# Loads of 62 KB a partition, V cut to fill them, and K one head ahead near the end, in a DMA-fed decode kernel

## The chip, the cores and the metric

The kernel runs on one core of one Trainium2 chip. The metric is device time in microseconds (us), the median of several runs; lower is better.

## What is computed

One decode step, fp32 throughout, with two tokens (B = 2, one query each, D = 512). The input x is layer-normed to xn, and the result is the sum of three terms:

```python
def _A_ref(x, k_cache, v_cache, wq, wo):           # 32 heads of 128, window W = 2048
    q = (x @ wq).reshape(B, Sq, Hq, Dh).transpose(0, 2, 1, 3)
    k = k_cache[:, :, Sk - W:, :]; v = v_cache[:, :, Sk - W:, :]
    scores = einsum("bhqd,bhkd->bhqk", q, k) * (Dh ** -0.5)
    o = einsum("bhqk,bhkd->bhqd", softmax(scores), v)
    return o.transpose(0, 2, 1, 3).reshape(B, Sq, Hq * Dh) @ wo
def _B_ref(x, w_gate, w_up, w_down):               # F = 1376, no nonlinearity
    return ((x @ w_gate) * (x @ w_up)) @ w_down
return x + _A_ref(xn, ...) + _B_ref(xn, ...)
```

Only the last 2048 positions of the K and V caches are read. Every byte of K, V and the weights is used once.

## The kernel before, in words

**The stream.** Before the launch, all inputs but a small rest are laid out in one long array, `stream`, in the order in which they will be loaded. `blocks()` (line 47) is that order: a list of loads, each a list of fields, and each field a kind, an index and a width in fp32 elements a partition. The kinds are `k` and `v` (one head's K or V for both tokens, CK = 4096 elements, which is 16 KB a partition), `wq` (a quarter of the query weights of a group of four heads, 512), `wo` (one head's output weights, 512), `wg`/`wu` (gate and up weights, in two halves), `wd`, `wh` (chunks and half chunks of w_down, 512 and 256), `wr` (the x term and a few rest rows of w_down) and `vh` (one token's half of the last head's V).

**The buffers.** A load goes into a `step` tile of STEP elements a partition; STEP is three units of 4608, so 13,824 elements, 54 KB. There are three such buffers (`BUFS = 3`). `pump()` (line 150) issues the next load on SP as soon as a buffer is free in program order, and `done()` (line 173) strikes off a field when the instruction that uses it has been written; when the last field of a load is struck off, the buffer is free and `pump()` is called. On the chip the DMA instruction on SP then waits on the engines that read the old contents. A load of the steady part holds exactly three units, either K, V, K or V, K, V of successive heads with their `wq` and `wo`; V runs three heads behind K (LAG = 3). Loads that share a buffer's key at the end (the last V's and the w_down pieces) are separate DMAs into one buffer. The 25-row rest of w_down goes to the tile `wd_tail` by one more DMA on SP (line 187), issued behind the first three loads.

**One head.** For each K, VectorE (DVE) multiplies K by the broadcast query (`products`, line 278) and sums over the head dimension (`sums`, 286); `maxima` (291) takes the maximum on DVE and over the partitions on GpSimd (POOL); `weights` (299) makes the exponentials on ScalarE (ACT) and sums them on POOL; `reciprocals` (314) runs on DVE. For V, TensorE (PE) multiplies the weights with V (`weigh`, 330: 8 pieces of 512 columns, two matmul records for each, as fp32), ACT copies the sum out of PSUM (`copy_out`, 339), PE transposes it (`transpose`, 346) and ACT scales it into `oT`, and PE multiplies by `wo` into `acc` (`project_o`, 365). `pv` (373) does the weighing of one or two heads and the copy, `values` (379) the whole of it. PE also makes the queries of coming heads (`project_q`, 261) and the gate and up products (395). Each engine runs its instructions in the order written (class `InOrder`, whose line 102 therefore stands for nearly all instructions in the profile).

**The order.** The main loop (line 471) goes through the loads of `blocks()`: for each K of the load it does the head's work, and the `values` of the load's V heads come after the first K's sums. It breaks off ahead of the loads that hold V of head 27. Then the end is written out by hand (lines 496 to 548): head 30's products and sums, `values` of heads 26 and 27, head 31's products, then V of heads 28 to 31 as they land, with `down(n)` (432) for chunks of w_down, and `keep_busy(n)` (327), a matmul whose result nothing uses, in PE's waits. Line 508 puts a copy of the accumulator in a tile of its own, `acc_sb`, ahead of a new accumulation over four column groups. The last five loads are: half of V 31; `wo` 31 with w_down chunks 4 to 6; chunk 7 with the first half chunk; two half chunks; the last half chunk (`down_half`, 443). The result is copied by DVE (`o_out`) and written by one DMA.

Of the kernel before, what the change touches and what calls it, by code (L numbers as in the profile page):

```python
# [8 lines left out]
F32 = mybir.dt.float32  # L9
# [7 lines left out]
P = 128  # L17
B, D, H, DH, SK, F = 2, 512, 32, 128, 8192, 1376
# [6 lines left out]
FR = F - NFC * P  # L25
FH = [(0, 2 * FB), (2 * FB, F)]
LAG = 3
M = B
OUT = P

# [2 lines left out]
JG = J // 4  # L33
CK, CQ, CO = B * J * DH, NC * GC, D
CP = CQ // NC
UNIT = CK + max(CP, CO)
STEP = 3 * UNIT
WD = [(0, 2), (2, 4), (4, 7), (7, 8)]
HD = D // 2
HP = P // 2  # L40
NT, FT, FP = 2, 25, 28
FX = FR - NT * FT
RX = M + FX
PADS = 96, 248


def blocks():

    def wd(n):
        return [("wd", i, D) for i in range(*WD[n])]

    def k(h):
        return [("k", h, CK)] + ([("wq", h, CP)] if h + HG < H else [])  # L60

    def v(h):
        return [("v", h, CK), ("wo", h, CO)]

    def gu(half):
        n = NC * (FH[half][1] - FH[half][0])
        return [("wg", half, n), ("wu", half, n)]

    units = []
    for h in range(LAG, H - 1):  # L70
        units += [k(h), v(h - LAG)]
    ones = [("pick", 0, 8 * B), ("rows", 0, NFB * B)]
    first = [("x", 0, B * NC)] + ones + [("w", 0, NC * DH)]
    loads = [[("w", 1, CQ - NC * DH)] + k(0) + k(1), gu(0) + k(2)]
    loads += [gu(1) + units[0] + units[1] + wd(0) + [("wr", 0, HD)]]
    loads += [sum(units[i : i + 3], []) for i in range(2, len(units), 3)]
    loads += [k(H - 1) + v(H - 1 - LAG) + wd(1)]
    out = [(("f", 0), first)] + [(("s", i), fields) for i, fields in enumerate(loads)]
    late, last = ("s", len(loads)), ("s", len(loads) + 1)
    out += [(late, v(H - 3) + [("vh", 0, CK // B)]), (late, v(H - 2))]  # L80
    out += [(last, [("vh", 1, CK // B)]), (last, [("wo", H - 1, CO)] + wd(2))]
    halves = [("wh", (c, n), HD) for c in range(WD[-1][1], NFC) for n in range(2)]
    out += [(last, wd(3) + halves[:1])]
    return out + [(last, halves[i : i + 2]) for i in range(1, len(halves), 2)]


class InOrder:
# [30 lines left out]
def kernel(  # L118
# [65 lines left out]
    pick = got["pick", 0][0].rearrange("p (r s b) -> p r s b", s=2, b=B)  # L184
    rows = got["rows", 0][0]

    sp.dma_start(wd_tail[FP : FP + FT, :], tail)
    carry = rows[:M, :M]

    mean_w = const.tile([P, P], F32, name="mean_w")  # L190
# [43 lines left out]
        xnb, xn.rearrange("p c b -> p (c b)").unsqueeze(2).to_broadcast([P, NC * B, P])  # L234
    )

    q_ps, s_t, mm_t, p_t, sum_t, rec_t, o_sbs, oT = {}, {}, {}, {}, {}, {}, {}, {}
    n_acc = bank = 0

    def side(h):  # L240
# [89 lines left out]
    def weigh(h, v, parts, first, last):  # L330

        for n, part in enumerate(parts):
            b, i = divmod(part, JG)
            pe.matmul(
                o_ps[bank][32 * i : 32 * i + 8 * B, :], p_t[h][:, b, i, :],
                v[:, FB * n : FB * (n + 1)], start=first and b == 0, stop=last and b == B - 1,
            )

    def copy_out():
        nonlocal bank  # L340
        o_sb = small.tile([P, 4 * DH], F32, name="o_sb", bufs=2)
        act.copy(o_sb, o_ps[bank])
        bank = 1 - bank
        return o_sb

    def transpose(heads, o_sb):
        d = tr[:, 8 + 4 * bank : 12 + 4 * bank]
# [24 lines left out]

    def pv(heads):
        for h in heads:
            weigh(h, got["v", h][0], range(CK // FB), h == heads[0], h == heads[-1])
            done("v", h)
        return copy_out()

    def values(heads, busy=((), ())):
        o_sb = pv(heads)  # L380
        for n in busy[0]:
            keep_busy(n)
        transpose(heads, o_sb)
        for n in busy[1]:
            keep_busy(n)
        for h in heads:
            project_o(h)

# [79 lines left out]
    spare_in = xnb.rearrange("p a b -> p (a b)")  # L468
    for i in range(2):
        project_first(i)  # L470
    for _, fields in blocks():
        ks = [i for kind, i, _ in fields if kind == "k"]
        vs = [i for kind, i, _ in fields if kind == "v"]
        if vs and vs[-1] >= H - 5:
            break
# [26 lines left out]
    maxima(h)  # L502
    reciprocals(h - 1)
# [24 lines left out]
    project_o(H - 3)  # L528
    reciprocals(h + 1)
    keep_busy(P)  # L530
    weigh(H - 2, got["v", H - 2][0], range(CK // FB), False, False)
    done("v", H - 2)
    keep_busy(192)
    weigh(H - 1, got["vh", 1][0], range(JG, B * JG), False, True)
    done("vh", 1)
# [17 lines left out]
def laid_out(x):  # L553
# [29 lines left out]
    def field(kind, i):  # L583
        if kind in first:
            return first[kind]
        if kind in ("k", "v"):
            return cache[kind][i].reshape(P, CK)
        if kind == "w":
# [56 lines left out]
```

## Time and profile before

| what | value |
|---|---|
| time, median of 3 runs | 377.35 us (377.3 to 377.47) |
| the profiled execution's own time | 377.36 us |
| its span, first to last instruction | 375.5 us |
| mean granted TensorE clock | 0.805 |
| PE, DVE, ACT, POOL busy | 256.6, 294.5, 58.2, 25.2 us |
| read from HBM | 159.50 MB |

The profile is one execution. Its busy shares are averages over the whole span. The DMA share of a stretch is the mean busy share of the core's 16 DMA engines. A packet row counts every transfer that a DMA engine made, data and the 4-byte semaphore writes behind it. The "us to landing" of an issue runs from the start of the instruction on SP to the last engine's end of that load, so it includes the time in the queue behind earlier loads. PEld is the weight load of a matmul; where matmuls follow closely, its start times are the finer clock of PE's progress.

### The profile page before, as it was taken

To read this page: it belongs to the slowest core of one execution; us is meant where nothing else is said; L and a number is where in the kernel's file an instruction comes from. 1 tells how busy PE (TensorE), PEld (TensorE's weight loads), DVE (VectorE), ACT (ScalarE), POOL (GpSimd) and SP (SyncE) were. 2 spreads that over 40 slices of the span, in tenths; PEclk is the share of its full clock that TensorE was granted. 3 is DMA by queue.
4 is the path that set the end of the run, shared out by engine and by line. 5 is a ranking of instruction groups with operands and counts; after the bars stand their busy time and mean duration, and the time that the engine had idled before them with its cause. 6 is when DMAs were issued, how large, how long until landed. Compare 5 with 4: busy or idle time off the path is not lost.

```text
span 375.5 us, 2881 instructions
## 1 busy us (share of the span) xinstructions
PE 256.6 (68%) x1100; PEld 87.3 (23%) x1100; DVE 294.5 (78%) x145; ACT 58.2 (16%) x260; POOL 25.2 (7%) x74
## 2 busy tenths in 40 slices
PE   3386586988648486854858675385847768646996
PEld 3241123232112122211222122121212123012343
DVE  4299691998599499869949976994997799599950
ACT  1011002122020211201112020111202021121131
POOL 1001000000000000000000100000000000000010
PEclk9996988889896666889766698875869688556999
DMA  8999999999999999999999999999999999999995
GB/s 323 468 436 450 401 440 442 412 459 427 425 442 418 448 442 412 443 430 436 448 407 449 430 424 454 414 443 436 418 459 418 432 445 431 430 420 435 418 413 237
DMA packets 4506, 159.73 MB, mean 425 GB/s; under 512 B 501, under 2 KB 757, under 8 KB 1166
## 3 DMA queue, kind: packets, MB, share of 16 engines
q1 hardware_dynamic: 4494, 159.57, 98.6%
q8 instruction: 8, 0.13, 0.1%
q14 instruction: 4, 0.03, 0.0%
HBM read 159.50 MB, written 0.07 MB: 425 GB/s over the span
## 4 chain that ended last, share of the span: by engine, by line
DMA 62%; PE 18%; DVE 17%; ACT 2%; issue 1%; SPq 0%; DVEq 0%
DMA step<-in_stream_dram 62%; DVE step L102 8%; DVE s L102 8%; PE o_ps L102 6%; PE q L102 4%; PE acc L102 4%; PE tr L102 3%; ACT o_sb L102 1%; ACT oT L102 1%; SPq L102 0%; ACT hT L102 0%; DVE o_sb L102 0%; DVE m L102 0%; ACT hX L102 0%; DVE o_out L102 0%
## 5 line engine op out<-in xcount | busy, mean ns | idle before, releaser
L102 DVE TENSOR_TENSOR step<-step,q 128x4096 f32<-128x4096 f32 x31 | 136.6, 4407 | 53.2 <-DMA step<-in_stream_dram 53.2
L102 PE MATMUL q<-step,xnb 128*128 128x512 f32 (+1 forms) x128 | 93.0, 877 | 74.8 <-DMA step<-in_stream_dram 74.8
L102 DVE TENSOR_REDUCE s<-step 128x32 f32<-128x4096 f32 x32 | 141.4, 4419 | 1.1
L102 PE MATMUL o_ps<-step,p 128*16 128x512 f32 x512 | 69.8, 680 | 10.3 <-DMA step<-in_stream_dram 10.3
L102 PEld LDWEIGHTS q<-step,xnb 128*128 128x128 f32 x128 | 32.5, 276 | 129.4 <-DMA step<-in_stream_dram 75.3
L102 PE MATMUL acc<-step,oT 128*2 128x512 f32 (+1 forms) x88 | 35.1, 553 | 9.1 <-ACT oT L102 9.1
L102 PE MATMUL tr<-first,o_sb 128*128 128x2 f32 (+4 forms) x192 | 26.6, 257 | 15.9 <-ACT o_sb L102 12.8
L102 ACT COPY o_sb<-o_ps 128x512 f32<-128x512 f32 x23 | 13.5, 585 | 149.2 <-PE o_ps L102 149.2
L102 PEld LDWEIGHTS tr<-first,o_sb 128*128 128x128 f32 (+2 forms) x192 | 24.2, 195 | 37.0 <-ACT o_sb L102 31.8
L296 POOL PARTITION_ALL_REDUCE mm<-m x32 | 11.3, 354 | 282.9 <-DVE rec L102 177.7
L102 PEld LDWEIGHTS o_ps<-step,p 128*16 128x16 f32 x512 | 13.3, 106 | 70.3 <-issue 53.3
L102 ACT ACTIVATE nm<-mm 128x2 f32<-128x2 f32 x32 | 6.5, 203 | 126.2 <-POOL mm L296 126.2
L102 ACT ACTIVATE p<-s,nm 128x16 f32<-128x16 f32 x64 | 19.2, 300 | 1.0
L312 POOL PARTITION_ALL_REDUCE sum<-rs x32 | 12.7, 398 | 55.5 <-ACT p L102 55.5
L102 ACT ACTIVATE oT<-tr,rec 128x1 f32<-128x1 f32 x64 | 12.1, 260 | 26.6 <-PE tr L102 26.6
L102 PE MATMUL o_ps<-step,xn 128*2 128x512 f32 (+1 forms) x48 | 12.6, 575 | 0.0
L102 DVE TENSOR_TENSOR step<-step,tr 128x4096 f32<-128x4096 f32 x1 | 4.4, 4421 | 9.6 <-DMA step<-in_stream_dram 9.6
L102 ACT ACTIVATION_READ_ACCUMULATOR p<-s,nm 128x1 f32 x64 | 11.9, 186 | 0.0
L102 PE MATMUL q<-xnb,mean_w 128*128 128x512 f32 (+4 forms) x24 | 9.4, 487 | 0.0
L102 PEld LDWEIGHTS acc<-step,oT 128*2 128x2 f32 x88 | 3.9, 83 | 18.7 <-ACT oT L102 14.5
L102 PE MATMUL acc<-step,hT 128*2 128x128 f32 (+2 forms) x72 | 7.1, 306 | 0.0
L102 DVE COPY o_out<-acc 128x128 f32<-128x128 f32 x1 | 0.3, 292 | 8.5 <-PE acc L102 8.5
(40 smaller groups left out, 44.3 us busy)
## 6 DMA issues: line engine op xcount, KB each, us to landing
step<-in_stream_dram SPq DMA_DIRECT2D x16, 6912.0 KB, 33.6
step<-in_stream_dram SPq DMA_DIRECT2D x2, 6656.0 KB, 37.2
step<-in_stream_dram SPq DMA_DIRECT2D x2, 6400.0 KB, 32.8
step<-in_stream_dram SPq DMA_DIRECT2D x1, 5376.0 KB, 15.5
step<-in_stream_dram SPq DMA_DIRECT2D x1, 4864.0 KB, 29.8
step<-in_stream_dram SPq DMA_DIRECT2D x1, 3328.0 KB, 16.9
step<-in_stream_dram SPq DMA_DIRECT2D x1, 2304.0 KB, 22.0
step<-in_stream_dram SPq DMA_DIRECT2D x2, 1024.0 KB, 16.8
```

Of the source, the lines that this page charges most:

```text
L102: made = call(*args, **kwargs)
L296: nc.gpsimd.partition_all_reduce(mm, m, P, bass_isa.ReduceOp.max)
L312: nc.gpsimd.partition_all_reduce(sum_t[h], rs, P, bass_isa.ReduceOp.add)
```

## The change

- STEP is 31 blocks of 512 elements: 15,872 elements, 62 KB a partition (63,488 bytes). The three buffers stay three.
- A new function `packed` fills each steady load to exactly STEP. It takes fields from the queue in order, skips one that doesn't fit for a later one that does, and cuts a V (in pieces of 512 columns) where only a part fits. A field of kind `v` is now keyed by head and range of pieces; `weigh_all` multiplies the pieces of one head, and strikes each off by itself.
- From head EARLY = 27 on, K goes one place earlier in the order of the stream; `groups()` writes the loop's order of heads apart from the loads, and `values` of the group with head 27 comes at the group's end. Heads 28 and 29 get a loop of their own, and V of head 25 moves to the part written by hand, where `transpose` gets a `slot`.
- The first loads are put together anew: queries and K 0, 1, 2; gate and up weights with K 3; V 0, w_down and K 4, V 1.
- At the end, chunk 7 of w_down and three half chunks are one load (5,120 bytes a partition) in place of two (3,072 and 2,048); `project_o` of head 30 goes ahead of `down(3)`. Of the calls of `keep_busy` around V of heads 26 and 27, two of 512 columns fall away.
- `wd_tail` is loaded by five DMAs of five rows in place of one of 25, and `acc_sb` takes a buffer of the `o_sb` pool.

The loads by bytes a partition: before 2,168 (first), 43,008, 51,200, 53,248, sixteen of 55,296, 51,200, 53,248, 38,912, 26,624, 18,432, 8,192, 8,192, 3,072, 2,048, 1,024: 30 loads. After: 2,168, 61,440, 62,464, 60,416, fifteen of 63,488, 38,912, 26,624, 18,432, 8,192, 8,192, 5,120, 1,024: 26 loads. Both sum to 1,245,304 bytes a partition. After, ten V heads are cut in two (3, 7, 8, 10, 12, 15, 19, 22, 23, 25).

```diff
-UNIT = CK + max(CP, CO)
-STEP = 3 * UNIT
+BLK = CO
+STEP = 31 * BLK
...
+def packed(queue):
+    loads = []
+    while queue:
+        load, room = [], STEP
+        while queue and room:
+            n = next((n for n, f in enumerate(queue) if f[2] <= room or f[0] == "v"), None)
+            if n is None:
+                break
+            kind, i, w = queue.pop(n)
+            if w > room:
+                h, p0, p1 = i
+                cut = p0 + room // FB
+                queue.insert(n, (kind, (h, cut, p1), (p1 - cut) * FB))
+                i, w = (h, p0, cut), room
+            load.append((kind, i, w))
+            room -= w
+        loads.append(load)
+    return loads
+
+def groups():
+    units = [u for h in range(LAG, H - 1) for u in (("k", h), ("v", h - LAG))]
+    parts = [[("k", 0), ("k", 1)], [("k", 2)], units[:2]]
+    parts += [units[i : i + 3] for i in range(2, len(units), 3)]
+    return [[[i for kind, i in p if kind == want] for want in "kv"] for p in parts]
...
-    loads = [[("w", 1, CQ - NC * DH)] + k(0) + k(1), gu(0) + k(2)]
-    loads += [gu(1) + units[0] + units[1] + wd(0) + [("wr", 0, HD)]]
-    loads += [sum(units[i : i + 3], []) for i in range(2, len(units), 3)]
+    loads = [[("w", 1, CQ - NC * DH)] + k(0) + k(1) + k(2), gu(0) + k(3) + gu(1)]
+    loads += [v(0) + wd(0) + [("wr", 0, HD)] + k(LAG + 1) + v(1)]
+    order = [(h - (h >= EARLY), k, h) for h in range(LAG + 2, H - 1)]
+    order += [(h + 0.5, v, h - LAG) for h in range(LAG + 2, H - 1)]
+    order.sort(key=lambda n: n[0])
+    loads += packed([f for _, fields, h in order for f in fields(h)])
...
-    out += [(last, wd(3) + halves[:1])]
-    return out + [(last, halves[i : i + 2]) for i in range(1, len(halves), 2)]
+    return out + [(last, wd(3) + halves[:-1]), (last, halves[-1:])]
...
-    sp.dma_start(wd_tail[FP : FP + FT, :], tail)
+    for i in range(0, FT, FT // TS):
+        sp.dma_start(wd_tail[FP + i : FP + i + FT // TS, :], tail[i : i + FT // TS, :])
...
+    def weigh_all(h, first, last):
+        for kind, i in [key for key in got if key[0] == "v" and key[1][0] == h]:
+            weigh(h, got[kind, i][0], range(i[1], i[2]), first, last)
+            done(kind, i)
...
-            if vs and n == 0:
+            if vs and n == 0 and h < EARLY:
                 values(vs)
...
+            if h == EARLY:
+                values(vs)
+
+    for h in (H - 4, H - 3):
+        products(h)
+        sums(h)
+        maxima(h)
+        weights(h)
+        reciprocals(h - 1)
...
-    values([H - 6, H - 5], ((GC, 256), (GC,)))
+    o_sbs = pv([H - 7]), pv([H - 6, H - 5])
+    transpose([H - 7], o_sbs[0], 1 - bank)
+    transpose([H - 6, H - 5], o_sbs[1])
+    keep_busy(256)
+    for i in range(H - 7, HF):
+        project_o(i)
     keep_busy(GC)
...
-    acc_sb = const.tile([M, D], F32, name="acc_sb")
+    acc_sb = small.tile([P, D], F32, name="o_sb", bufs=2)[:M, :]
...
     down(2)
     project_o(H - 1)
+    project_o(H - 2)
     down(3)
-    project_o(H - 2)
```

More of the change, by code (lines that the diff above doesn't have):

```diff
@@ L27 @@
 LAG = 3
+EARLY = 27
 M = B
@@ L40 @@
 HP = P // 2
-NT, FT, FP = 2, 25, 28
+NT, FT, FP, TS = 2, 25, 28, 5
 FX = FR - NT * FT
@@ L44, with k, v @@
 PADS = 96, 248
+def k(h):
+    return [("k", h, CK)] + ([("wq", h, CP)] if h + HG < H else [])
+def v(h):
+    return [("v", (h, 0, CK // FB), CK), ("wo", h, CO)]
+def packed(queue):
[21 more added lines that the diff above has]
+    return [[[i for kind, i in p if kind == want] for want in "kv"] for p in parts]
 def blocks():
@@ L57, in wd @@
         return [("wd", i, D) for i in range(*WD[n])]
[L59 to L63, printed above, removed]
     def gu(half):
@@ L67, in gu @@
         return [("wg", half, n), ("wu", half, n)]
-    units = []
-    for h in range(LAG, H - 1):
-        units += [k(h), v(h - LAG)]
     ones = [("pick", 0, 8 * B), ("rows", 0, NFB * B)]
     first = [("x", 0, B * NC)] + ones + [("w", 0, NC * DH)]
-    loads = [[("w", 1, CQ - NC * DH)] + k(0) + k(1), gu(0) + k(2)]
-    loads += [gu(1) + units[0] + units[1] + wd(0) + [("wr", 0, HD)]]
-    loads += [sum(units[i : i + 3], []) for i in range(2, len(units), 3)]
+    loads = [[("w", 1, CQ - NC * DH)] + k(0) + k(1) + k(2), gu(0) + k(3) + gu(1)]
[4 more added lines that the diff above has]
+    loads += packed([f for _, fields, h in order for f in fields(h)])
     loads += [k(H - 1) + v(H - 1 - LAG) + wd(1)]
@@ L235 @@
     )
-    q_ps, s_t, mm_t, p_t, sum_t, rec_t, o_sbs, oT = {}, {}, {}, {}, {}, {}, {}, {}
+    q_ps, s_t, mm_t, p_t, sum_t, rec_t, oT = {}, {}, {}, {}, {}, {}, {}
     n_acc = bank = 0
@@ L344, in copy_out, with transpose @@
         return o_sb
-    def transpose(heads, o_sb):
-        d = tr[:, 8 + 4 * bank : 12 + 4 * bank]
+    def transpose(heads, o_sb, slot=None):
+        slot = bank if slot is None else slot
+        d = tr[:, 8 + 4 * slot : 12 + 4 * slot]
         s0, s1 = side(heads[0]), side(heads[-1]) + 1
@@ L374, in pv, with values @@
         for h in heads:
-            weigh(h, got["v", h][0], range(CK // FB), h == heads[0], h == heads[-1])
-            done("v", h)
+            weigh_all(h, h == heads[0], h == heads[-1])
         return copy_out()
[L379 to L385, printed above, removed]
+    def values(heads):
+        transpose(heads, pv(heads))
         for h in heads:
@@ L470 @@
         project_first(i)
[L471 to L475, printed above, removed]
+    for ks, vs in groups()[:-2]:
         for n, h in enumerate(ks):
@@ L530 @@
     keep_busy(P)
-    weigh(H - 2, got["v", H - 2][0], range(CK // FB), False, False)
-    done("v", H - 2)
+    weigh_all(H - 2, False, False)
     keep_busy(192)
@@ L585, in field @@
             return first[kind]
-        if kind in ("k", "v"):
+        if kind == "k":
             return cache[kind][i].reshape(P, CK)
+        if kind == "v":
+            h, p0, p1 = i
+            return cache[kind][h].reshape(P, CK)[:, p0 * FB : p1 * FB]
         if kind == "w":
```

## The prediction, as it stood before the result

> **What bounds the kernel now.** I read the page's strip of slices and its DMA queues first. The DMA line holds nine tenths or more from the second slice to the last but one, and one hardware queue takes nearly all of the span.
>
> ```profile
> span 375.5 us, 2881 instructions
> DMA  8999999999999999999999999999999999999995
> q1 hardware_dynamic: 4494, 159.57, 98.6%
> DMA 62%; PE 18%; DVE 17%; ACT 2%; issue 1%; SPq 0%; DVEq 0%
> ```
>
> A mean can hide holes, so I cut the span into windows (busy us of PE, PEld, DVE, ACT, POOL, then clock, DMA share, GB/s), and asked the DMA view for the even stretch from 130 to 310 us, where only 54 KB loads are in flight, and for the last small loads.
>
> ```profile
> 20.00:60.00 40.00, 28.42 (x86) 9.66 (x84) 33.37 (x16) 5.30 (x22) 2.61 (x7) 0.87 1.00 430
> 100.00:140.00 40.00, 26.37 (x109) 7.94 (x108) 34.20 (x17) 5.98 (x26) 2.36 (x7) 0.76 0.99 430
> 300.00:340.00 40.00, 24.54 (x92) 7.85 (x88) 35.58 (x17) 6.88 (x31) 3.01 (x8) 0.67 0.98 425
> ```
>
> ```profile
> DMA packets 1597, 78.19 MB, mean 434 GB/s; under 512 B 177, under 2 KB 177, under 8 KB 177
> q1 hardware_dynamic: 1591, 78.10, 100.2%
> ...
> DMA packets 489, 1.14 MB, mean 254 GB/s; under 512 B 63, under 2 KB 191, under 8 KB 445
> q1 hardware_dynamic: 489, 1.14, 64.7%
> ```
>
> The reader is to see that the 16 engines never run dry: shares of 0.98 to 1.00, 434 GB/s. DVE, the next engine, is busy 33 to 36 of 40 us and spends its idle time on loads. So the time is: about 2 us until data flows, the stream, what follows the last bytes (3 us to the span's end), and 377.36 - 375.5 = 1.86 us around the span. The profiled execution stands 0.01 us over the median, so I take its times as they are. Bytes don't change (1,245,304 a partition in both lists). What can change is the cost of cutting them into loads, a hole in the stream, and the end.
>
> **Fewer loads.** A load is 128 row transfers and 16 semaphore writes, so 8 and 1 on each engine. What a packet costs beside its bytes comes from the two DMA answers. In the even stretch (180 us, 16 engines) 78.10 MB took 1.002 x 2880 = 2885.8 engine-us, 36.95 us a MB. In the last stretch (368.5 to 373 us) 489 packets took 0.647 x 72 = 46.6 engine-us, of which 1.14 MB explain 42.1; 4.5 us over 489 packets is 9 ns each. Four stream loads fewer are 36 packets fewer on every engine: 0.3 us. A 63,488-byte row is paid by its bytes, as 55,296 ones are. Bounds: nothing, if the 9 ns lies in the shape of the last stretch, or 0.65 us if all that the windows leave (0.01 of 40 us over 2.5 load boundaries, 0.16 us each) is a pause at each boundary; I take 0.3, the row that measures packets. The Trainium skill, "DMA: Bandwidth & Descriptors", section "Anatomy of one DMA — SWDGE (gpsimd) path", gives a fixed cost of about 2.0 us for each DMA beside bytes over 436 GB/s, measured for GpSimd's own; by that four loads would be worth 8 us. The trace disagrees for loads queued behind one another: 2 us at 2.5 boundaries would be a share of 0.88 in each window, not 0.98 to 1.00.
>
> **The rest of w_down in five DMAs.** No view shows over how many engines its 25 rows go. The 100 KB (last row below) are 3.8 engine-us at 36.95 us a MB: 0.24 us on each of 16, 3.8 on one. A spread other than today's could move the last engine by -0.5 us (from five engines to all) or +3. I take no change, the value in between: the rows, their size and their queue stay as they are. Four more semaphore writes (0.04 us) stand against the 0.3. The Trainium skill, same page, section "Why a DMA increments its semaphore by 16 and not by 1", says that the largest number up to 16 which divides the rows is the number of engines, the lowest-numbered ones: five for 25 rows and for 5. No row here shows it.
>
> **Do larger buffers arrive too late?** SP waits for the buffer, mostly for K's sums:
>
> ```profile
> SPq L102 <- DVE s L102: 306.9, 21, 31.7
> 34.70 9.38 SPq L102 DMA_DIRECT2D step<-in_stream_dram  x2
> step<-in_stream_dram SPq DMA_DIRECT2D x16, 6912.0 KB, 33.6
> L102 DVE TENSOR_TENSOR step<-step,tr x1: 4421/4421/4421, 16.7 to 16.7; 128x4096 f32<-128x4096 f32 x1
> 83.30 4.40 DVE L102 TENSOR_TENSOR step<-step,q 128x4096 f32<-128x4096 f32 x1
> 87.73 4.42 DVE L102 TENSOR_REDUCE s<-step 128x32 f32<-128x4096 f32 x1
> 92.19 0.19 DVE L102 TENSOR_REDUCE m<-s 128x2 f32<-128x32 f32 x1
> wd_tail<-in_tail_dram SPq DMA_DIRECT2D x1, 100.0 KB
> ```
>
> A 6,912 KB load needs 16.3 us at 434 GB/s and lands 33.6 us after its issue: it has waited 17 us in the queue, which is the spare time of the issue. A K head costs DVE 9.1 us (83.30 to 92.4). After, the tightest place is the start. The first load is 18,432 bytes a partition longer, 5.4 us, so the first product goes from 16.7 to about 22.1; three heads end near 49.5 and free the buffer. The three first loads hold 184,320 bytes a partition, 54.4 us, so the queue is fed to about 57.5: 8 us to spare. In the steady part a load lasts 18.7 us and holds at most two K heads, 18.2 us of DVE. Where a V is cut, the first piece keeps its buffer until the next load has landed, but PE does not queue behind those K sums: query products, weighing and projection are some 5 to 7 us, out of 18.7. Near the end the early K frees its buffers sooner. So the stream keeps its pace; this edit costs and brings nothing. A hole would cost what an issue is late, below 8 us at the first place, most likely nothing.
>
> **The end.** Here are PE, ACT, DVE and SP rows (start, duration) of the run-up and of the end, from 368.07 on, where the second half of V 31 has landed, and the landings of the last loads:
>
> ```profile
> 348.12 1.10 PE L102 MATMUL q<-xnb,mean_w 128*128 128x512 f32 x2
> 349.15 1.88 PE L102 MATMUL acc<-step,oT 128*2 128x512 f32 x4
> 352.28 1.91 PE L102 MATMUL o_ps<-step,p 128*16 128x512 f32 x16 [0.19 <-DMA step<-in_stream_dram]
> 360.15 1.91 PE L102 MATMUL o_ps<-step,p 128*16 128x512 f32 x16 [0.28 <-DMA step<-in_stream_dram]
> 368.07 0.13 PEld L102 LDWEIGHTS o_ps<-step,p 128*16 128x16 f32 x8 [0.24 <-DMA step<-in_stream_dram]
> 370.93 0.72 ACT L102 ACTIVATE oT<-tr,rec 128x1 f32<-128x1 f32 x4 [1.15 <-PE tr L102]
> 371.39 0.19 PEld L102 LDWEIGHTS acc<-step,oT 128*2 128x2 f32 x8
> 371.58 0.21 PEld L102 LDWEIGHTS acc<-step,hT 128*2 128x2 f32 x8
> 371.80 0.21 PEld L102 LDWEIGHTS acc<-step,oT 128*2 128x2 f32 x8
> 372.02 0.55 PEld L102 LDWEIGHTS acc<-step,hT 128*2 128x2 f32 x32
> 372.82 0.29 DVE L102 COPY o_out<-acc 128x128 f32<-128x128 f32 x1 [8.52 <-PE acc L102]
> ...
> 353.10 0.90 SPq L102 DMA_DIRECT2D step<-in_stream_dram  x2
> 354.04 0.43 SPq L102 DMA_DIRECT2D step<-in_stream_dram  x1
> step<-in_stream_dram SPq DMA_DIRECT2D x1, 256.0 KB, 18.5
> step<-in_stream_dram SPq DMA_DIRECT2D x1, 128.0 KB, 18.4
> ```
>
> The last load (128 KB) lands at 354.04 + 18.4 = 372.4, and the last eight of PE's 32 weight loads run at about 372.46: PE comes to it as it lands. The load before it (256 KB, issued at 353.57) lands near 372.1, and PE has its first 24 half-chunk matmuls behind it by then. So two chains end together: PE's from 368.07, and the stream's. After, PE's chain up to the projections is 0.2 us earlier (three loads fewer ahead of it). But chunk 7 and three half chunks now land together, where the 256 KB load did: 372.1 less 0.3, at 371.8. PE needs chunk 7 at 371.58 today. With `project_o` of head 30 ahead of it (ready when ACT has made its oT, 371.65 today, 371.45 after) PE is done with both projections near 371.65 and waits to 371.85. Then come chunk 7 (0.22 us) and four half chunks (0.5): the weight loads end at 371.85 + 0.72 = 372.57, as today (372.02 + 0.55). The 0.3 us of the stream is thus spent waiting for the merged load: sum -0.05 us, between -0.3 (PE doesn't wait) and +0.1.
>
> In the run-up PE gets half a V head more (8 of the 16 matmuls of 1.91 us, 0.95), one transpose (1.05, row below) and one projection (half of 1.88), and loses two keep-busy calls of 512 columns (1.10 each, the row at 348.12). The surplus of 0.7 us stands against idle times of 0.19 and 0.28 us ahead of the next two V heads and the 0.2 us by which PE starts earlier, so V 28 may start 0.3 us late against its data, and V 29 is level again. DVE gets head 30 before it needs it and starts head 31 at its landing; it is not last.
>
> **Rivals.** (a) *The saving goes through to the end*: PE doesn't wait for the merged load, 377.35 - 0.3 = 377.05. For it: PE and the stream are level to 0.05 us; against it: the working above. (b) *A pause at every load boundary*, or a better spread of the rest rows: -0.65 to -0.8, 376.6, and 369.3 by the skill's 2 us. The windows speak against it. (c) *Slower: an instruction fetch meets the last engine.* The program's own instructions come over the same engines:
>
> ```profile
> DMA  6959593959695979394989695989997887776631
> q8 instruction: 1, 0.02, 1.0%
> q8 instruction: 8, 0.13, 0.1%
> ```
>
> The first two rows are of 366 to 372 us: one fetch there took 1.0% of 96 engine-us, 0.96 us on one engine, and the strip of slices shows that the engines finish as much as 2 us apart. A load counts as landed with its last engine. If one of the eight fetches falls to the engine that is last, instead of one that is early, all of the end moves by 0.9: 378.2. It decides when the delays of one engine sum to more than today's last. Nothing in the change steers it. (d) *The clock drops in the run-up.* With less keep-busy, the end may run at half clock, as this shows from 320 to 340 us (sixteen V matmuls 3.62 against 1.91 us, a transpose 1.87 against 1.05):
>
> ```profile
> 325.13 3.62 PE L102 MATMUL o_ps<-step,p 128*16 128x512 f32 x16 [2.74 <-DMA step<-in_stream_dram]
> 329.45 1.87 PE L102 MATMUL tr<-first,o_sb 128*128 128x2 f32 x8 [0.70 <-ACT o_sb L102]
> 355.81 1.05 PE L102 MATMUL tr<-first,o_sb 128*128 128x2 f32 x8
> ```
>
> Behind 368.07 that would add 0.9, 0.8 and some 1.5 us: 380.5. Against it: PE has no idle time over 0.3 us there. (e) *A hole in the stream*, an issue late by 2 us: 379.4.
>
> **How the numbers follow.** The forecast, level within 0.1 us of before, has 0.57; (a) 0.17; (b) 0.08; (c) 0.10; (d) 0.05; (e) 0.03. A measurement of this kernel can tell about 0.2% from no change, 0.75 us. Faster by more holds (b), 0.08; the same holds the forecast and (a), 0.74; slower (c), (d), (e), 0.18. Predicted 377.3 us. The range from 376.8 (under (a), with part of the packet cost's upper bound) to 378.3 (with (c)) holds 0.84.
>
> **What would show it.** Right: stretches of 40 us at 0.98 to 1.00 in the DMA share; 25 step loads; the last load landing 0.3 us earlier; PE's weight loads idle for about 0.2 us on DMA ahead of chunk 7, with no wait ahead of the last half chunk; the o_out copy at 372.8. Wrong: a DMA share under 0.97 anywhere before 366 us, SP issues that come after the queue is empty, a clock of 0.5 after 350 us, or o_out off by more than 0.5 us.

## The result, and the profile after

The changed kernel takes 379.48 us in the median of 18 runs, the kernel before 377.38 beside it (18 runs, 377.07 to 378.42). Two of the 18 runs of after, at 384.12 and 387.12 us, lie far above the rest (378.35 to 380.23); the ratios, and the medians from here on, leave such runs out. That gives 379.33 us for after, 2.0 us or 0.5% slower, ratio 1.0049 with a 95% interval of 1.0039 to 1.0058. The forecast was 377.3 us, the range ended at 378.3, and slower had a chance of 0.18. The profiled execution of after took 379.92 us, 0.6 above that median, so its own difference to the one of before, 2.56 us, is a little more than the typical one.

The page of after first, the same four lines as before:

```profile
span 378.1 us, 2875 instructions
...
DMA  8999999999999999999999999999999999999993
...
q1 hardware_dynamic: 3938, 159.57, 97.8%
...
DMA 61%; DVE 19%; PE 17%; ACT 1%; issue 0%; SPq 0%; DVEq 0%
```

It looks as before: the engines are full to the last slice, there are 556 packets fewer (4 loads of 144 fewer, and 20 more for the small DMAs), and q1's share falls by 0.8 points because the span is longer: 97.8% of 378.1 us and 98.6% of 375.5 are both 370 us. The windows of 40 us (PE, PEld, DVE, ACT, POOL, clock, DMA share, GB/s), the even stretch from 130 to 310 us in the DMA view, and DVE's first product say the same:

```profile
20.00:60.00 40.00, 29.99 (x84) 10.37 (x84) 36.53 (x16) 4.87 (x19) 2.61 (x7) 0.91 0.98 422
100.00:140.00 40.00, 33.37 (x124) 11.31 (x124) 29.76 (x14) 7.35 (x36) 2.66 (x7) 0.77 1.01 437
300.00:340.00 40.00, 22.44 (x87) 6.30 (x86) 38.80 (x17) 5.77 (x28) 3.01 (x8) 0.79 0.99 431
```

```profile
DMA packets 1396, 78.17 MB, mean 434 GB/s; under 512 B 160, under 2 KB 160, under 8 KB 160
...
q1 hardware_dynamic: 1390, 78.09, 100.2%
```

```profile
22.13 4.42 DVE L126 TENSOR_TENSOR step<-step,tr 128x4096 f32<-128x4096 f32 x1 [15.03 <-DMA step<-in_stream_dram]
```

So the larger buffers did what the prediction said: no gap, the same 434 GB/s, the first product at 22.1 us. The time was lost elsewhere, and the chain of waits shows where. Its last pieces (start, duration, what) are, before:

```profile
343.19 16.92 DMA step<-in_stream_dram
360.15 1.91 PE o_ps L102 x16
...
370.89 1.91 PE acc L102 x80
```

and after:

```profile
303.27 37.99 DMA step<-in_stream_dram
341.31 7.20 PE o_ps L126 x40
...
355.31 1.84 PE o_ps L126 x16
...
362.83 1.84 PE o_ps L126 x16
...
373.48 1.92 PE acc L126 x80
```

The reader is to see the place where DMA leaves the chain. Before, the stream carries it to 360.15 us, and PE works off what landed. After, the stream is last at 341.31; from there the end is 34 us of PE work, one piece behind the other, with one wait of 0.50 us for ACT. The page's share (DMA 62% against 61%) shows nothing of it. PE's rows of that stretch, the run-up to V 28, before (the rows between 348 and 353 us stand in the prediction):

```profile
340.81 5.17 PE L102 MATMUL o_ps<-step,p 128*16 128x512 f32 x32 [7.12 <-DMA step<-in_stream_dram]
345.91 1.56 PE L102 MATMUL q<-xnb,mean_w 128*128 128x512 f32 x4
347.31 0.95 PE L102 MATMUL tr<-first,o_sb 128*128 128x4 f32 x8
```

and after, to V 28 (355.24), V 29 (362.76) and the output:

```profile
341.31 7.20 PE L126 MATMUL o_ps<-step,p 128*16 128x512 f32 x40 [7.45 <-DMA step<-in_stream_dram]
348.44 1.05 PE L126 MATMUL tr<-first,o_sb 128*128 128x2 f32 x8
349.99 1.05 PE L126 MATMUL tr<-first,o_sb 128*128 128x4 f32 x8 [0.50 <-ACT oT L126]
350.91 0.68 PE L126 MATMUL q<-xnb,mean_w 128*128 128x256 f32 x2
351.51 2.74 PE L126 MATMUL acc<-step,oT 128*2 128x512 f32 x6
354.18 1.13 PE L126 MATMUL q<-xnb,mean_w 128*128 128x512 f32 x2
355.24 1.91 PE L126 MATMUL o_ps<-step,p 128*16 128x512 f32 x16
...
362.76 1.91 PE L126 MATMUL o_ps<-step,p 128*16 128x512 f32 x16
...
375.42 0.29 DVE L126 COPY o_out<-acc 128x128 f32<-128x128 f32 x1 [8.51 <-PE acc L126]
...
375.74 0.35 SPq L126 DMA_DIRECT2D out_dram<-o_out  x1
```

V 28 and V 29 wait for no DMA now: the brackets that stood there before, 0.19 and 0.28 us, are gone. An engine that never waits for data is the one that sets the end. The stream was done before: a DMA view of 368.5 to 373.2 us in 40 slices shows the last bytes in the 34th, by 372.5 us, 3.2 us ahead of the output's issue at 375.74.

```profile
GB/s 340 279 619 410 366 383 410 523 383 288 479 471 262 506 410 357 366 253 305 401 261 331 148 288 261 148 166 113 122 78 0 17 26 26 0 0 0 0 0 0
```

The sum of the run-up, after against before: PE starts 0.50 us later (341.31 - 340.81), the V matmuls take 2.03 more (7.20 - 5.17), and what lies between them and V 28 takes 0.62 more: 355.24 - 348.44 = 6.80 against 352.28 - 0.19 - 345.91 = 6.18. That makes 3.15, of which the first 0.50 is later data and the rest PE's own; V 28 had 0.19 of waiting to give, so it starts 2.96 later. From V 28 to the copy of the result PE needs 20.18 us when nothing waits (375.42 - 355.24), and 20.54 before (372.82 - 352.28), 0.36 more, for waits. 2.96 - 0.36 = 2.60, the shift of the copy.

Why the V matmuls take 2.03 us more for 8 matmuls: the granted clock. Windows of 3.4 us with the same columns as above, before:

```profile
339.60:343.00 3.40, 2.19 (x12) 0.49 (x16) 3.40 (x1) 0.00 (x0) 0.00 (x0) 0.50 1.01 435
343.00:346.40 3.40, 3.40 (x25) 0.79 (x18) 3.37 (x4) 1.24 (x6) 0.75 (x2) 0.86 1.06 458
```

and after:

```profile
339.60:343.00 3.40, 1.69 (x10) 0.33 (x14) 2.96 (x4) 0.90 (x5) 0.75 (x2) 0.50 0.98 423
343.00:346.40 3.40, 3.40 (x20) 0.66 (x16) 3.37 (x2) 0.58 (x1) 0.00 (x0) 0.50 1.06 458
346.40:349.80 3.40, 3.09 (x28) 1.35 (x20) 3.40 (x1) 0.86 (x3) 0.00 (x0) 0.94 0.93 394
```

PE comes to the run-up out of 7 us of idle time, at a clock of 0.50. If the clock is either 0.50 or 1.00, a mean of 0.86 in the second window of before means that full speed came 1 us into it, near 344.0; after it came 0.4 us into the third (0.94), near 346.8. So PE ran 5.5 of the 7.1 us of its V matmuls at half clock, and 3.2 of 5.1 before. The Trainium skill, "TensorE: Matmul & The Clock Gate", section "Part 1: The HAM clock gate (the "warmup" mystery)", says that the gate halves the clock after an idle window and raises it after a busy one, and that the windows of 3413 ns run freely and don't start anew with the kernel; the trace agrees in kind, as the wake-up comes 3.2 us behind PE's start in one execution and 5.5 in the other, but these 2.3 us are more than the 500 ns either way that the section gives for the transition.

### The profile page after: what moved, and what is told of

Read it like the earlier page. It is cut to its first block, busy times and chain, and to the rows that moved or that the text cites. A ratio compares the mean times of both kernels' runs of the same rounds, so it can differ in the third digit from the quotient of the medians.

```text
span 378.1 us, 2875 instructions
## 1 busy us (share of the span) xinstructions
PE 257.4 (68%) x1096; PEld 88.2 (23%) x1096; DVE 295.4 (78%) x145; ACT 57.2 (15%) x260; POOL 25.2 (7%) x74
## 3 DMA queue, kind: packets, MB, share of 16 engines
q1 hardware_dynamic: 3938, 159.57, 97.8%
## 4 chain that ended last, share of the span: by engine, by line
DMA 61%; DVE 19%; PE 17%; ACT 1%; issue 0%; SPq 0%; DVEq 0%
DMA step<-in_stream_dram 61%; DVE s L126 9%; DVE step L126 9%; PE o_ps L126 6%; PE acc L126 4%; PE q L126 4%; PE tr L126 3%; ACT o_sb L126 1%; ACT oT L126 0%; DVE m L126 0%; SPq L126 0%; DVE o_out L126 0%; DVE rec L126 0%; DVEq L126 0%
## 5 line engine op out<-in xcount | busy, mean ns | idle before, releaser
L126 PE MATMUL o_ps<-step,p 128*16 128x512 f32 x512 | 81.5, 693 | 50.0 <-DMA step<-in_stream_dram 49.9
L126 PE MATMUL q<-step,xnb 128*128 128x512 f32 (+1 forms) x128 | 77.2, 754 | 31.7 <-DMA step<-in_stream_dram 31.7
L126 PEld LDWEIGHTS q<-step,xnb 128*128 128x128 f32 x128 | 29.5, 246 | 83.2 <-issue 67.8
L126 PE MATMUL acc<-step,oT 128*2 128x512 f32 (+1 forms) x88 | 38.3, 597 | 8.5 <-ACT oT L126 8.5
L126 PE MATMUL tr<-first,o_sb 128*128 128x2 f32 (+4 forms) x192 | 29.8, 274 | 15.7 <-ACT o_sb L126 11.8
L126 PEld LDWEIGHTS o_ps<-step,p 128*16 128x16 f32 x512 | 14.3, 103 | 106.1 <-DMA step<-in_stream_dram 58.6
L126 PEld LDWEIGHTS tr<-first,o_sb 128*128 128x128 f32 (+2 forms) x192 | 27.1, 216 | 40.4 <-ACT o_sb L126 34.3
L126 PE MATMUL o_ps<-step,xn 128*2 128x512 f32 (+1 forms) x48 | 14.9, 682 | 5.9 <-DMA step<-in_stream_dram 5.9
L126 DVE RECIPROCAL rec<-sum 128x2 f32<-128x2 f32 x32 | 5.0, 155 | 4.2 <-POOL sum L337 4.2
L126 PE MATMUL q<-xnb,mean_w 128*128 128x512 f32 (+4 forms) x20 | 7.4, 461 | 0.0
```

The costliest lines, as they stand in the source:

```text
L126: made = call(*args, **kwargs)
```

## The experiments

**Theory P**: PE's chain of the run-up sets the end. The change put half a V head, a transpose and a projection into it, at a time of half clock, and PE had some 0.5 us to spare. **Rival S**: the stream ends later (five small DMAs, other loads), and PE is late because its data is. **Rival M**: the merged load and the order of projections at the end cost more than was worked out. Twelve kernels were run, each beside the kernel before on the same chip. The last three columns are of the one profiled run of each: what the V matmuls behind the landing of V 26 and 27 took, the start of V 28 (before 352.28), and "o_out", the start of the result's copy (before 372.82).

| kernel | median us | before | ratio [95%] | V matmuls us | V 28 | o_out |
|---|---|---|---|---|---|---|
| after | 379.33 | 377.38 | 1.0049 [1.0039, 1.0058] | 7.20 (x40) | 355.24 | 375.42 |
| e1_warm | 379.41 | 377.33 | 1.0066 [1.0036, 1.0096] | 6.99 (x40) | 354.90 | 375.08 |
| e2_no_busy | 377.87 | 377.33 | 1.0010 [0.9994, 1.0025] | 7.28 (x40) | 352.90 | 373.93 |
| e3_tail_one | 379.75 | 377.33 | 1.0054 [1.0033, 1.0075] | 7.16 (x40) | 355.01 | 375.19 |
| e4_old_end | 379.07 | 377.33 | 1.0041 [1.0023, 1.0058] | 5.23 (x32) | 354.31 | 375.47 |
| e5_warm8 | 378.51 | 377.36 | 1.0023 [1.0002, 1.0043] | 4.49 (x40) | 353.94 | 374.12 |
| e6_before_busy | 378.78 | 377.36 | 1.0025 [0.9998, 1.0052] | 5.77 (x32) | 354.04 | 374.22 |
| e7_before_merge | 377.42 | 377.36 | 0.9995 [0.9977, 1.0013] | 5.47 (x32) | 352.19 | 372.89 |
| e8_before_tail5 | 378.18 | 377.36 | 1.0014 [0.9996, 1.0032] | 5.77 (x32) | 353.27 | 373.47 |
| e9_lean | 377.74 | 377.61 | 1.0004 [0.9994, 1.0015] | 5.87 (x40) | 352.13 | 372.84 |
| e10_loads_alone | 377.78 | 377.61 | 1.0010 [0.9987, 1.0033] | 6.53 (x32) | 353.24 | 373.42 |
| e11_before_no_busy | 377.24 | 377.61 | 0.9990 [0.9978, 1.0002] | 5.17 (x32) | 352.07 | 372.62 |
| e12_loads_no_busy | 377.3 | 377.2 | 1.0002 [0.9992, 1.0011] | 6.00 (x32) | 351.90 | 372.41 |

The last two columns carry most of the verdict. In after, e1, e3, e5, e6, e8 and e10, o_out stands 20.18 to 20.20 us behind V 28: from there PE waits for no data, and a late V 28 is paid in full. In e2 the profile records three V matmuls ahead of the last projection, at 352.90; counted back from the row behind them as in after (1.72 us), V 28 starts at 353.75, and o_out is again 20.18 us behind it.

**e1_warm**: four `keep_busy` between the two pieces of V 25, to raise the clock before the run-up.

```diff
-    o_sbs = pv([H - 7]), pv([H - 6, H - 5])
+    p0, p1 = sorted(i for kind, i in got if kind == "v" and i[0] == H - 7)
+    weigh(H - 7, got["v", p0][0], range(p0[1], p0[2]), True, False)
+    done("v", p0)
+    for _ in range(4):
+        keep_busy(GC)
+    weigh(H - 7, got["v", p1][0], range(p1[1], p1[2]), False, True)
+    done("v", p1)
+    o_sbs = copy_out(), pv([H - 6, H - 5])
```

> The changed kernel with four keep-busy matmul calls of 512 columns between the two pieces of V 25, so that PE works while it waits for the load with the second piece. Theory P (PE's run-up ahead of V 28 is what is late: 40 V matmuls at half clock and more work than before): clock 1.0 from about 341 us on, the 40 V matmuls take 4.3 us in place of 7.2, V 28 starts within 0.3 us of its data, and the time is 377.2 to 377.9, with less spread between runs than the 1.9 us of the changed kernel. Rival D (the stream's last engine lands later, 372.85 against 372.41): the time stays at 379.0 to 379.9.

379.41 us: nothing moved. The cure was too small to reach the place.

```profile
341.18 6.99 PE L126 MATMUL o_ps<-step,p 128*16 128x512 f32 x40 [4.02 <-DMA step<-in_stream_dram]
```

The calls ended 4.02 us before the data, and the V matmuls are as long as in after: the clock was down again when they began. It says nothing for or against P.

**e2_no_busy**: the `keep_busy(256)` and `keep_busy(GC)` of the run-up left out.

```diff
-    keep_busy(256)
...
-    keep_busy(GC)
```

> The changed kernel without the two keep-busy calls (256 and 512 columns) between the landing of V 26 and 27 and the weighing of V 28. Theory P: PE comes to V 28 1.3 us earlier (0.43 and 0.86), and the time falls by 1.0 to 1.3 us, to about 378.2. Rival D: no change, 379.5. If the calls are needed to hold the clock, the time rises by 1 us or more.

377.87 us, 1.5 less than after, for 1.8 us of PE work (0.68 + 1.13) that nothing uses. The profiled run, 378.45, is the slowest of its 11, and its o_out comes 1.49 earlier than after's. S is out as the whole cause: the loads are those of after.

**e3_tail_one**: after with one DMA for the rest of w_down.

```diff
-    for i in range(0, FT, FT // TS):
-        sp.dma_start(wd_tail[FP + i : FP + i + FT // TS, :], tail[i : i + FT // TS, :])
+    sp.dma_start(wd_tail[FP : FP + FT, :], tail)
```

> The changed kernel with the 25 rest rows of w_down in one DMA again. Theory P: the time stays within 0.3 us of 379.5, as PE is late, whatever the stream does; the first 62 KB rows behind the rest rows lose the extra 0.3 us that they took on 15 engines at 57.5 us, and the last load lands 0.3 us earlier. Rival D: the time follows the last landing, 0.3 to 0.5 us down.

379.75 us, as after. What the stream gets back here (the V matmuls start at 341.12 in place of 341.31) is not seen while PE is 2 us late behind it.

**e4_old_end**: the 62 KB loads with the orders of before in the end.

```diff
-    order = [(h - (h >= EARLY), k, h) for h in range(LAG + 2, H - 1)]
-    order += [(h + 0.5, v, h - LAG) for h in range(LAG + 2, H - 1)]
+    order = [(h, k, h) for h in range(LAG + 2, H - 4)]
+    order += [(h + 0.5, v, h - LAG) for h in range(LAG + 2, H - 4)]
...
+    loads += [k(H - 4) + v(H - 7) + k(H - 3), v(H - 6) + k(H - 2) + v(H - 5)]
```

> 62 KB loads with V in pieces up to K 27 and V 24, and behind them the loads and the order of before (K 28, V 25, K 29; V 26, K 30, V 27) with before's keep-busy calls, so that V 25 is weighed, transposed and projected ahead of the run-up; the merged w_down load and the five small DMAs stay. Theory P: V 28 starts within 0.3 us of its data, time 377.0 to 377.6. Rival L (the larger loads or cut V cost by themselves): the time stays over 378.5.

379.07 us, for a reason of its own. The packing left one short load (22 KB a partition), and the buffer behind it came free only with the projections of a V (SP waits 11.0 us for PE's `acc`): the DMA view from 320 to 327 us shows the engines run dry,

```profile
DMA  6099699900666696660000000990707000070009
```

and SP's timeline the next issue, which comes only at 323.49:

```profile
323.49 1.19 SPq L127 DMA_DIRECT2D step<-in_stream_dram  x2
```

V 28 waits for its data here (0.39 us). It is rival (e) of the prediction, made by the experiment: about 2 us. As a test of P it failed; e10 takes its place.

**e5_warm8**: as e1, with eight calls.

```diff
-    for _ in range(4):
+    for _ in range(8):
```

> As the run with four keep-busy calls between the two pieces of V 25, with eight: there the calls ended at 337.2 us, PE stood idle for 4.0 us, and the clock was back at 0.5 when the load landed at 341.2, so the remedy had not been applied. Theory P (late run-up at half clock): idle under 1.5 us ahead of the landing, clock 1.0 behind it, the 40 V matmuls in 4.3 to 5 us in place of 7.2, V 28 within 0.3 us of its data, time 377.5 to 378.0 (then set by the last landing near 372.85). If the clock stays at 0.5 in spite of the calls, the time stays at 379 to 380. Rival (PE's extra work alone, without the clock): at most 0.5 us gained.

378.51 us, 0.8 less than after, but not the 377.5 to 378.0 that was expected. PE's rows:

```profile
341.02 4.49 PE L126 MATMUL o_ps<-step,p 128*16 128x512 f32 x40 [0.91 <-DMA step<-in_stream_dram]
...
348.52 4.43 PE L126 MATMUL acc<-step,oT 128*2 128x512 f32 x6
```

The forty V matmuls take 4.49 us at full clock, against 7.20: the half clock cost after 2.7 us in this one place. Part of it came back: the clock fell again, and the six projections took 4.43 instead of 2.74, so V 28 starts only 1.3 us earlier than in after.

**e6_before_busy**: the kernel before, with two `keep_busy(GC)` more in the run-up, 1.7 us by their rows.

```diff
-    values([H - 6, H - 5], ((GC, 256), (GC,)))
+    values([H - 6, H - 5], ((GC, 256), (GC, GC, GC)))
```

> The kernel before with two more keep-busy calls of 512 columns in its run-up, behind the transposes of heads 26 and 27: 1.7 us of PE work, which stands for the surplus of the changed kernel's run-up. Theory P: PE's chain from there to the end has 0.2 + 0.3 + 0.2 us of waits on data to absorb it, the rest comes out at the end: 378.3 to 378.5, with no waits on DMA ahead of V 28, V 29 and the second half of V 31. If the end is set by the stream alone: no change, 377.4.

378.78 us, 1.4 more than before and a little more than expected, with the loads and the stream of before. V 28 starts at 354.04 with no wait. Useless columns in that place, and nothing else, do to the old kernel more than half of what the change did; the interval of the ratio just reaches 1.

**e7_before_merge**: the kernel before with the merged w_down load and the projections in the new order.

```diff
-    out += [(last, wd(3) + halves[:1])]
-    return out + [(last, halves[i : i + 2]) for i in range(1, len(halves), 2)]
+    return out + [(last, wd(3) + halves[:-1]), (last, halves[-1:])]
...
-    down(3)
     project_o(H - 2)
+    down(3)
```

> The kernel before with the merged w_down load and the order of the last projections from the change, and nothing else. The prediction's working: PE waits about 0.2 us for the merged load and comes to the last half chunk 0.1 us late; time 377.35 to 377.55. If PE waits for nothing, 377.2 to 377.3.

377.42 against 377.36 us: level, within 0.2% by the interval. M is out.

```profile
371.97 0.66 PEld L101 LDWEIGHTS acc<-step,hT 128*2 128x2 f32 x40 [0.30 <-DMA step<-in_stream_dram]
...
372.89 0.29 DVE L101 COPY o_out<-acc 128x128 f32<-128x128 f32 x1 [8.70 <-PE acc L101]
```

PE does wait for the merged load ahead of chunk 7, 0.30 us, and gets it back in the closer row of 40 weight loads, as the prediction worked it out.

**e8_before_tail5**: the kernel before, with the rest of w_down in five DMAs.

```diff
-    sp.dma_start(wd_tail[FP : FP + FT, :], tail)
+    for i in range(0, FT, 5):
+        sp.dma_start(wd_tail[FP + i : FP + i + 5, :], tail[i : i + 5, :])
```

> The kernel before with the rest rows of w_down in five DMAs of five rows, and nothing else. The changed kernel's first rows behind them took some 0.3 us longer on 15 engines, and not with one DMA of 25 rows: so the stream and the time are 0.3 us later, 377.6 to 377.7. By the prediction's working (four more semaphore writes): no change, 377.4.

378.18 us, 0.8 over before and more than the 377.6 to 377.7 that was expected (the interval of the ratio, 0.9996 to 1.0032, still holds 1). The DMA view around these rows, 45.5 to 48.5 us, of before and then of e8:

```profile
q1 hardware_dynamic: 62, 0.99, 78.1%
```

```profile
q1 hardware_dynamic: 82, 0.99, 89.7%
```

The same 0.99 MB and 20 packets more take 11.6% of 48 engine-us more, 5.6 engine-us or 0.35 us on each engine. By the 9 ns a packet of the prediction it would have been 0.2 engine-us. PE's V matmuls start at 341.46, 0.65 later than before, and V 28 at 353.27, 1.0 later. But the small DMAs are not shown to be the reason for all of that. DVE's starts behind a wait for data, in before and then in e8:

```profile
228.44 4.42 DVE L102 TENSOR_TENSOR step<-step,q 128x4096 f32<-128x4096 f32 x1 [5.30 <-DMA step<-in_stream_dram]
...
261.17 4.42 DVE L102 TENSOR_TENSOR step<-step,q 128x4096 f32<-128x4096 f32 x1 [5.43 <-DMA step<-in_stream_dram]
```

```profile
228.60 4.42 DVE L102 TENSOR_TENSOR step<-step,q 128x4096 f32<-128x4096 f32 x1 [5.30 <-DMA step<-in_stream_dram]
...
261.81 4.42 DVE L102 TENSOR_TENSOR step<-step,q 128x4096 f32<-128x4096 f32 x1 [5.92 <-DMA step<-in_stream_dram]
```

At 228 us e8 is 0.16 late, at 261 us 0.64, and no small DMA runs in between. Nearly the same step, 0.45 us, lies between e3 (228.28, then 266.31) and e9 (228.29, then 265.86), which have the same loads and one DMA; what makes it is not shown. V 28 is later still because the V matmuls took 5.77 us, as they did in e6 with one DMA, in place of 5.17.

**e9_lean**: after with one DMA for the rest, without three keep-busy calls (256 and GC in the run-up, GC behind the transpose of head 28).

```diff
-    for i in range(0, FT, FT // TS):
-        sp.dma_start(wd_tail[FP + i : FP + i + FT // TS, :], tail[i : i + FT // TS, :])
+    sp.dma_start(wd_tail[FP : FP + FT, :], tail)
...
-    keep_busy(256)
...
-    keep_busy(GC)
...
-    keep_busy(GC)
```

> The changed kernel with the rest rows in one DMA, without the keep-busy calls of 256 and 512 columns in the run-up, and without the one of 512 columns behind the transpose of head 28: 2.1 us less of PE work behind the landing of V 26 and 27. Theory P: PE has caught up by V 29, waits on DMA appear again ahead of V 29 or later, and the end is that of the stream: last landing near 372.6, time 377.2 to 377.7. If lateness elsewhere is at work, over 378.

377.74 against 377.61 us, just over the range that was expected: the loss is gone, with all the large loads, the early K and the extra V work still in place.

```profile
352.13 1.91 PE L126 MATMUL o_ps<-step,p 128*16 128x512 f32 x16 [0.39 <-DMA step<-in_stream_dram]
...
360.01 1.91 PE L126 MATMUL o_ps<-step,p 128*16 128x512 f32 x16 [0.66 <-DMA step<-in_stream_dram]
```

The waits for DMA are back in the brackets: the stream sets the end again.

**e10_loads_alone**: the large buffers and first loads, the packing to 60 KB up to K 26 and V 22, and from V 23 on the loads, the order and the end of before, one DMA for the rest (28 stream loads).

```diff
-        load, room = [], STEP
+        load, room = [], 30 * BLK
...
-    order = [(h - (h >= EARLY), k, h) for h in range(LAG + 2, H - 1)]
-    order += [(h + 0.5, v, h - LAG) for h in range(LAG + 2, H - 1)]
+    order = [(h, k, h) for h in range(LAG + 2, H - 5)]
+    order += [(h + 0.5, v, h - LAG) for h in range(LAG + 2, H - 6)]
...
+    loads += [v(H - 9) + k(H - 5) + v(H - 8)]
+    loads += [k(H - 4) + v(H - 7) + k(H - 3), v(H - 6) + k(H - 2) + v(H - 5)]
```

> The changed first loads and loads of 60 to 62 KB with V in pieces up to K 26 and V 22, then the loads, the order, the keep-busy calls and the end of before from V 23 on, no short load between, the rest rows in one DMA and the w_down loads as before: two loads fewer than before. Theory P: the larger loads cost nothing by themselves: no hole in the stream, V 28 within 0.3 us of its data, 377.1 to 377.5. Rival L (larger loads or cut V cost by themselves): over 378.

377.78 against 377.61 us, not to be told from before, though above the 377.1 to 377.5 that was expected. In the profiled run V 28 starts at 353.24 with no wait, 1.0 us later than before, since the V matmuls took 6.53 us. The larger loads by themselves neither cost nor bring anything that these runs can see; the interval reaches from 0.5 us less to 1.2 us more.

**e11_before_no_busy**: the kernel before without any of the four run-up calls.

```diff
-    values([H - 6, H - 5], ((GC, 256), (GC,)))
-    keep_busy(GC)
+    values([H - 6, H - 5])
```

> The kernel before without its keep-busy calls between the landing of V 26 and 27 and V 28 (two calls of 512, one of 256 and one more of 512 columns). If before is held by the stream, PE has 3 us of idle there and the time stays at 377.4, or rises by 1 us or more if the clock falls back to 0.5 behind 350 us. If PE were late in before as well, the time would fall.

377.24 against 377.61 us (ratio 0.9990, 0.9978 to 1.0002).

```profile
352.07 1.91 PE L102 MATMUL o_ps<-step,p 128*16 128x512 f32 x16 [2.15 <-DMA step<-in_stream_dram]
```

Without the calls PE waits 2.15 us for V 28, and the V matmuls behind that wait still take 1.91 us: the clock held. So the calls keep nothing warm in this execution (e12 shows that this is not always so), and they are 3.8 us of PE time (1.56 + 1.10 + 1.12 by the rows of before).

**e12_loads_no_busy**: e10 without the four calls, the version that could have beaten both.

```diff
-    keep_busy(GC)
-    keep_busy(256)
     transpose([H - 6, H - 5], o_sb)
-    keep_busy(GC)
     for i in (H - 6, H - 5):
         project_o(i)
-    keep_busy(GC)
```

> The kernel of e10 (62 KB buffers, loads packed to 60 KB, the end of the kernel before, one wd_tail DMA) without the four keep-busy calls of the run-up. Theory (PE's chain of the run-up sets the end): e10 lost 0.60 us in its profiled run to a half clock in the run-up, with 2.8 us of keep-busy columns behind it that nothing needs; without them V 28 waits for its data again (DMA wait over 0.3 us), o_out lies within 0.4 us of 372.6 and the time is 377.0 to 377.4, 0.1 to 0.2% under the kernel before if the two step loads fewer count. Rival (larger loads cost something of their own): 377.8 again, with DMA waits ahead of V 28 and the last landing at 372.4 or later.

377.3 against 377.2 us (1.0002, 0.9992 to 1.0011): level with before. It doesn't beat it. In the profiled run the wait ahead of V 28 that was expected isn't there, since the clock took the time:

```profile
348.69 3.54 PE L129 MATMUL acc<-step,oT 128*2 128x512 f32 x4 [0.50 <-ACT oT L129]
351.90 2.05 PE L129 MATMUL o_ps<-step,p 128*16 128x512 f32 x16
```

Four projections at half clock took 3.54 us instead of 1.88.

## Why the prediction was wrong, point by point

**The failed step** is the last paragraph on the end: "The surplus of 0.7 us stands against idle times of 0.19 and 0.28 us [...], so V 28 may start 0.3 us late against its data, and V 29 is level again." V 28 started 2.96 us later than before and V 29 2.61, neither with a wait for data. The mechanism, more PE work against small waits, was the right one; three terms of the sum were mis-sized.

- *Half a V head, 0.95 us.* It was priced with the 1.91 us of V 28, a row at full clock, though it was put behind 7.12 us of idle time, where the rows are at half clock. Measured: 2.03. Not all of this is the change: the half clock lasts differently long from execution to execution. In the eight profiled runs with 32 matmuls they took 5.17 to 6.53 us (mean 5.64), and the profile of before, 5.17, is with e11's the shortest of them; in the four with 40 and no warming (after, e2, e3, e9) 5.87 to 7.28 (mean 6.88). The typical difference is about 1.2 us.
- *Transposes, projection and keep-busy calls, -0.2 us.* The working was 1.05 + 0.94 - 2.20. Measured: +0.62. The second transpose waits 0.50 us for ACT's `oT` (the bracket at 349.99), which was not counted, and the calls gave back 1.90, not 2.20, as the rows of neighbours overlap (from start to start they take 1.66 after and 3.56 before).
- *PE starts 0.2 us earlier.* It started 0.50 later. The gain of fewer loads was taken as certain, and the small DMAs as free. Executions differ by about as much: e3 and e9, with the same loads and one DMA, start at 341.12 and 340.66.

The 0.47 us of waits were the whole margin, and the sum as written already used it up; so whatever a term came out larger went straight to the end, 1 us for 1 us, which the step didn't say. With the typical 1.2 for 0.95, 0.6 for -0.2 and 0.5 for -0.2 the sum is 2.3, less about 0.5 of waits 1.8; measured in the median 2.0.

**Rival (d)** named the clock, with a chance of 0.05, and set it behind 368 us, where it was refuted by the lack of idle time. The clock was at full speed from 347 us on in after. It was the half clock that both kernels already have ahead of 347 us that counted, with more work put into it.

**The rest in five DMAs**, taken as no change, may be a second failure: alone it came with 0.8 us in the median (e8), inside the bounds that were given, -0.5 to +3. The interval allows 0, and in the profile 0.48 of the 0.64 us at 261 us arose far from the small DMAs. In the changed kernel what they cost is hidden behind PE (e3).

**Fewer loads, -0.3 us**: not shown. Where V 28 and V 29 wait for their data, they start at 352.13 and 360.01 with 26 loads (e9), at 352.07 and 359.93 with 30 (e11): no gain in these two executions. But the 0.46 us between e3 and e9 is more than the 0.3 that is looked for, so one execution of each can't rule it out. The 9 ns a packet may well lie in the shape of the last stretch, the lower bound.

**Larger buffers** (no hole, first product at 22.1, 25 step loads, shares of 0.98 to 1.01 in the windows shown) and **the merged load** (e7) came as worked out. Rivals (a) and (b) didn't happen, nor (e). Rival (c), an instruction fetch that meets the last engine, was not tested.

What stays open: how far the 1.9 us between the fastest and the slowest run of after is the clock's wake-up. The profiled runs fit it, with V matmuls between 5.87 and 7.28 us, but runs without a profile don't show their clock in the run-up.

## What to carry to other kernels

Where two chains end within half a microsecond of each other, a long stream hides the engine that is about to pass it: look in the chain of waits for the last point at which the stream leads, and count every instruction that a change puts behind it, each at the clock that its own place has. Work that is put right behind an idle time is priced by a row that stands behind an idle time. And a filler that is to keep the clock up costs PE time as soon as PE has no waits left, so it is the first thing to try without when real work arrives; e2 gained 1.5 us by it, and e12 shows the risk, a clock that falls in one execution.

## What the runs showed of the hardware that was not expected

**The clock can fall though PE was busy for most of the stretch ahead.** In e5 PE had just run its forty V matmuls at full speed; then came transposes with gaps of 0.5 us. Windows of 3.5 us:

```profile
345.50:349.00 3.50, 3.00 (x21) 2.23 (x21) 3.50 (x1) 1.71 (x7) 0.00 (x0) 1.00 1.10 472
349.00:352.50 3.50, 3.50 (x6) 0.42 (x4) 1.13 (x3) 0.00 (x0) 0.35 (x1) 0.51 0.89 384
```

PE was busy for 3.00 of 3.50 us in the first, and was granted half clock in the second. Of those 3.00 us 2.10 are transposes, whose matmuls move 2 or 4 columns each. Eight of them take 1.05 us, 0.13 each, about as long as a record of 512 columns (1.91 over 16, 0.12), so hardly any of that time is columns moving. That the clock gate takes such time for idle is a guess that no run here tests. In e11 a wait of 2.15 us did not lower the clock, and in e12 it fell behind waits of 0.72 and 0.50 us: the longest gap alone doesn't decide, and what does is open.

**Five small DMAs between large ones took more engine time than one**: five of 20 KB in place of one of 100 KB came with 0.35 us more packet time on each of the 16 engines (e8), for 20 packets more. How much of it reaches the end of the kernel is not shown.
